# Sliding-window attention and a two-layer network on one core: the first tiles of a half, steps 5 to 11, a mask and four loads are placed anew

## The chip, the cores and the metric

The kernel runs on one core of a Trainium2 chip. A core has five engines, each with its own queue of instructions in program order: TensorE (PE in the profile; its weight loads are shown apart as PEld), VectorE (DVE), ScalarE (ACT), GpSimd (POOL) and SyncE (SP). SP computes nothing here and only starts transfers; POOL starts some too. An engine does its instructions in order, and one that waits holds up all behind it. The metric is the device time of the kernel in microseconds (us), as a median of several runs.

## The reference

```python
def _attn_ref(q, k, v):                     # 8 batches, 8 heads, 576 tokens, 64 wide
    scores = scale * np.matmul(q, k.transpose(0, 1, 3, 2))
    mask = np.abs(pos[:, None] - pos[None, :]) <= 32
    scores = np.where(mask, scores, -1000000000.0)
    scores = scores - np.max(scores, axis=-1, keepdims=True)
    attn = np.exp(scores)
    attn = attn / (np.sum(attn, axis=-1, keepdims=True) + 1e-09)
    return np.matmul(attn, v)
...
def _moe_ref(x, w_in, w_out):               # x: 4608 x 512, d_ff 2048
    h = x @ w_in
    g = np.maximum(0.01 * h, h)
    return g @ w_out
```

Each token sees 65 neighbours at most. The heads of a token, side by side, are a row of x.

## The kernel before

Two heads make a pair: 4 pairs a batch, 8 batches, and each batch's 576 tokens are cut into two halves of 288. So there are 64 *steps*, numbered i; `where(i)` gives batch i // 8, half (i // 4) % 2 and pair i % 4. `g`, from 0 to 15, numbers the halves in the network.

**One step.** `score(i)` makes 5 matmuls (L276) into the one PSUM tile `ps`, ACT takes the exponent `e` out of it (L281), and POOL multiplies `e` with the mask of the half, `mask[0]` or `mask[1]`, into `prob` (L283). `sums(i)` adds up the keys by a matmul with ones (L302 where DVE has first joined two parts into `both`, L293, from step 12 on; L305, two matmuls, before), and DVE takes the reciprocal `r` (L310). `product(i)` makes 5 matmuls with the values (L321) into the one PSUM tile `x`, and DVE writes `xT`, x times r (L335). `step()` issues for step i, in this order: the join of i+1, the scores of i+2, sums, product and xT of i, and then what falls due: keys put in place (`place_keys`, DVE, L259 or L261), casts of q and k of a later batch (`cast_qk`, L198), their transposes by DMA (L213) and loads.

**Operands.** q, k and v come in fp32 as `qf`, `kf`, `vf`, one buffer for each pair, so a load waits for the cast of the batch before. Batches 0 and 1 are transposed by PE (`transposes`, L226) and taken out by ACT (L234, L240); later ones by DMA on SP's queue. The values of a pair are cast into `vbd`, of batch 1 by ACT (`cast_v` with `on_act`, L204, two instructions a pair), of later ones by POOL (L206). Keys go into `kbd`; both are double buffers by batch.

**Network.** `h_tile(g, f)` makes 4 matmuls (L349), one for each pair of heads c, into a PSUM tile of the pool `mm` (4 buffers), and ACT writes gT (L356). 16 tiles f make a half. `h_first` does the first four f at once, c by c, for g = 0 and 1. `o_tile(j)` makes 16 matmuls (L388) for 128 tokens, ACT copies them to `o_sb` (L393), SP stores them (L394).

**Order.** The order is written out by hand: up to step 7 and half g = 1 line by line, with `second_half()` for steps 4 to 7 between the tiles of g = 0, and `second_pair(p)`, which transposes pair p of batch 1 (on PE), between tiles of g = 1. From there a plan of quarter o tiles (4 matmuls, counted O_US = 0.864) and h tiles (H_US = 0.49) is walked through; `spend` is called before each piece and issues the next step when the planned clock has come to its `due` time. The plan opens with four o tiles (16 quarters, n = 0 to 15), then the 16 h tiles of g = 2. Before quarters 0 and 3 `spend` also calls `second_pair(2)` and `second_pair(3)`, and after the latter ACT casts the values of pair 0 of batch 1; the cast of pair i-7 goes out with step i for i = 8, 9, 10.

**Loads of a later batch.** In `step()` `qk_due` casts and transposes pair p of batch 2 in step 9 + p, of batch b > 2 in step 8 (b-1) + p + 2, and loads pair p of the batch after at once; `v_due` does the same for values.

```python
    LEAD = 4.0                                             # L566, with H_US and O_US
    due = []
    for i in range(8, NC):
        prev = 0.75 * O_US * 4 if i < 12 else at[i // 4 - 1] - LEAD + (1.8 if i < 16 else 0)
        due.append(prev + (at[i // 4] - LEAD + (1.8 if i < 12 else 0) - prev) * (i % 4 + 1) / 4)
```

`at[g]` is the planned time of the first h tile of half g. With these dues steps 8, 9, 10, 11 go out before the quarters n = 6, 9, 11 and 14.

Of the kernel before, what the change touches and what calls it, by code (L numbers as in the profile page):

```python
# [9 lines left out]
FP32 = mybir.dt.float32  # L10
# [6 lines left out]
def kernel(  # L17
# [14 lines left out]
    nc = tc.nc  # L32

    B, H, S, D = q.shape
# [5 lines left out]
    NPAIR = H // 2  # L40
    NB = S // 64
    HALF = S // 2
    DMC = DMODEL // 128
    FFC = DFF // 128
    EVEN = HALF // 2
# [12 lines left out]
    mmps = ctx.enter_context(tc.tile_pool(name="mmps", bufs=4, space=PS))  # L58
# [9 lines left out]
    def load_qk(b, p, behind=None):  # L68

        for into, src, name in ((qf, q, "qf"), (kf, k, "kf")):
            t = fload.tile([96, 2, RUN * D], FP32, name=f"{name}{p}")
            if behind is not None:
                behind.memset(t[0:1, 0, 0:1], 0.0)
                behind = None
            heads = src[b, 2 * p:2 * p + 2]
            if b < BY_DMA:
                nc.sync.dma_start(out=t, in_=heads.rearrange("a (p c) d -> p a (c d)", c=RUN))
            else:  # L80
                nc.sync.dma_start(
                    out=t.rearrange("p a (g e) -> p a g e", g=3),
                    in_=heads.rearrange("a (g p c) d -> p a g (c d)", g=3, c=2),
                )
            into[b, p] = t
# [45 lines left out]
    mask = [const.tile([128, 2, 2, EVEN], BF16, name=f"mask{i}") for i in range(2)]  # L131
# [16 lines left out]
    for lo in (0, 64):  # L148
        w = win[lo:lo + 64]
        nc.gpsimd.affine_select(  # L150
            out=w, in_=w, compare_op=ALU.is_ge, fill=0.0,
# [3 lines left out]
            out=w, in_=w, compare_op=ALU.is_ge, fill=0.0,  # L155
# [2 lines left out]
    nc.gpsimd.memset(vbd[0][:, 3], 0.0)  # L158
    win_f = win.rearrange("p c m i -> p c (m i)")

    def make_masks():
        for hf in range(2):
            lo = (16, 32)[hf]
            nc.gpsimd.tensor_copy(out=mask[hf][:, 0], in_=win_f[:, :, lo:lo + EVEN])
            lo = (16, 0)[hf]
            nc.gpsimd.tensor_copy(out=mask[hf][:, 1, :, lo:lo + 128], in_=win_f[:, :, 0:128])

    NPROB = 6
    prob = const.tile([128, NPROB, 2, 2, EVEN], BF16)
# [5 lines left out]
        out=ps[:, 512:512 + HALF], in_=zero.to_broadcast([128, HALF]), func=AF.Copy,  # L175
# [11 lines left out]
    def cast_qk(b, p, q_eng=None):  # L187
        for eng, src, dst in ((q_eng or nc.gpsimd, qf, qb), (nc.gpsimd, kf, kb)):
            if b < BY_DMA:
                parts = [(dst[:, p], src[b, p].rearrange("p a (c d) -> p c a d", d=D))]  # L190
            else:
                by_c = src[b, p].rearrange("p a (g c d) -> c p g a d", g=3, c=2)
                parts = [(dst[:, p, 3 * c:3 * c + 3], by_c[c]) for c in range(2)]
            for to, tok in parts:
                if eng is nc.scalar:
                    eng.activation(out=to, in_=tok, func=AF.Copy)
                else:
                    eng.tensor_copy(out=to, in_=tok)  # L198

    def cast_v(b, p, on_act=False):  # L200
        for a in range(2):
            r = slice(64 * a, 64 * a + 64)
            if on_act:
                nc.scalar.activation(out=vbd[b % 2][r, p, :, r], in_=vf[b, p][r], func=AF.Copy)  # L204
            else:
                nc.gpsimd.tensor_copy(out=vbd[b % 2][r, p, :, r], in_=vf[b, p][r])  # L206
# [42 lines left out]
    def place_keys():  # L249

        while landing and landing[0][0] <= state["done"]:
            unplaced.append(landing.pop(0)[1:])
        while unplaced:
            b, p, kT = unplaced.pop(0)
            for a in range(2):
                r = slice(64 * a, 64 * a + 64)
                to = kbd[b % 2][r, p, :, r]
                if b < BY_DMA:
                    nc.vector.tensor_copy(out=to, in_=kT[r].rearrange("p (n j) -> p n j", j=64))  # L259
                else:  # L260
                    nc.vector.tensor_copy(  # L261
                        out=to.rearrange("p n (m c) -> p n c m", c=2),
                        in_=kT[r].rearrange("p (c n m) -> p n c m", c=2, n=NB),
                    )
# [6 lines left out]
    def score(i):  # L271
        b, hf, p = where(i)
        by_c = qT[b][:, p].rearrange("p (c i) -> p c i", c=2)
        for n_, blocks in enumerate(WIN[hf]):
            for blk, i0, n in blocks:
                nc.tensor.matmul(  # L276
                    ps_v[:, n_, :, i0:i0 + n], kbd[b % 2][:, p, blk],
                    by_c[:, :, hf * EVEN + i0:hf * EVEN + i0 + n], start=True, stop=True,
                )
        e = attn.tile([128, 2 * HALF], BF16, name="e")  # L280
        nc.scalar.activation(out=e, in_=ps[:, P0:P0 + 2 * HALF], func=AF.Exp, scale=scale)  # L281
        pr = prob[:, i % NPROB]
        nc.gpsimd.tensor_mul(  # L283
            pr.rearrange("p n c i -> p (n c i)"), e, mask[hf].rearrange("p n c i -> p (n c i)"),
        )
        probs[i] = [pr, None, None]

    def join(i):


        pr = probs[i][0].rearrange("p n c i -> p n (c i)")
        both = joined.tile([128, HALF], BF16, name="both")
        nc.vector.tensor_add(both, pr[:, 0], pr[:, 1])  # L293
        probs[i][1] = both
# [42 lines left out]
    def weighted(i):  # L337
        if probs[i][2] is None:
            sums(i)
        product(i)  # L340
        scaled(i)
# [5 lines left out]
    def h_mms(g, f, h, cs):  # L347
        for c in cs:
            nc.tensor.matmul(  # L349
                h[:, 0:HALF], w_in_bf[:, c, ts(f, 128)], xT[:, c, ds(g * HALF % RING, HALF)],  # L350
                start=(c == 0), stop=(c == DMC - 1),
            )

    def h_out(g, f, h):

        nc.scalar.activation(  # L356
            out=gT[:, f, ds(g * HALF % RING, HALF)].rearrange("p (i c) -> p i c", c=2),
            in_=h[:, 0:HALF].rearrange("p (c i) -> p i c", c=2), func=AF.Prelu, alpha=0.01,
        )

    def h_tile(g, f):

        h = mmps.tile([128, 512], FP32, name="mm", tag="mm")
        h_mms(g, f, h, range(DMC))
        h_out(g, f, h)

    def h_first(g):

# [37 lines left out]
    NC = 2 * NPAIR * B  # L406
# [11 lines left out]
    def step():  # L418


        i = state["done"]
        if JOINED - 1 <= i < NC - 1:
            join(i + 1)
        if i < NC - 2:
            score(i + 2)
        weighted(i)
        place_keys()
        for b, p in qk_due.get(i, ()):
            cast_qk(b, p)
            transpose_dma(b, p)  # L430
            if b + 1 < B:
                load_qk(b + 1, p)
        for b, p in v_due.get(i, ()):
            cast_v(b, p)
            if b + 1 < B:
                load_v(b + 1, p)
        state["done"] += 1
# [5 lines left out]
    def load_w_in(f0, f1):  # L443
        nc.gpsimd.dma_start(out=w_in_bf[:, :, f0:f1], in_=w_in_r[:, :, f0:f1])
# [10 lines left out]
        place_keys()  # L455

    cast_qk(0, 0, nc.vector)
    make_masks()
    cast_qk(0, 1, nc.vector)
    first_pair()  # L460
    first_pair()
# [19 lines left out]
    next(first)  # L481
    cast_v(0, 1, on_act=True)
    load_w_in(1536, 2048)
    place_keys()
    keep_busy(ps, 0, 8)
    sums(2)
# [7 lines left out]
    h = next(h0)  # L494
# [34 lines left out]

    for f in range(4, FFC):  # L530
        h_tile(0, f)
        if f in (6, 10, 13):
            second_half()
        if f % 2 == 1:
            nc.gpsimd.memset((kbd if f < 12 else vbd)[1][:, (f - 4) // 2 % 4], 0.0)
# [30 lines left out]
    H_US, O_US, LEAD = 4 * (HALF / 2400 + 2.5e-3), 4 * 0.216, 4.0  # L566
# [8 lines left out]
    at, t = {}, 0.0  # L575
    for us, kind, g, f in plan:
        if kind == "h" and f == 0:
            at[g] = t
        t += us
    due = []  # L580
    for i in range(8, NC):
        prev = 0.75 * O_US * 4 if i < 12 else at[i // 4 - 1] - LEAD + (1.8 if i < 16 else 0)
        due.append(prev + (at[i // 4] - LEAD + (1.8 if i < 12 else 0) - prev) * (i % 4 + 1) / 4)
    clock = 0.0
    turn = 0

    def spend(us):
        nonlocal clock, turn
        while due and due[0] <= clock:
            due.pop(0)  # L590
            i = state["done"]
            if i < 11:
                cast_v(1, i - 7, on_act=True)
            step()
            if 10 <= i < 14:
                load_v(2, i - 10)
        turn += 1
        if turn == 1:
            second_pair(2)
        if turn == 2:  # L600
            score(9)
        if turn == 4:
            second_pair(3)
            cast_v(1, 0, on_act=True)
        clock += us

    for us, kind, g, f in plan:
        if kind == "h":
            spend(us)
            h_tile(g, f)  # L610
        elif f == 0:
            o_tile(g, lambda: spend(O_US))
# [28 lines left out]
```

## Time and profile before

| | |
|---|---|
| median of 9 runs | 321.02 us (320.43 to 321.72) |
| profiled execution | 321.11 us |
| its span, first to last instruction | 319.4 us |
| granted TensorE clock | 1.00 |
| DVE, share of the span | 69% |
| POOL, ACT, share of the span | 60%, 58% |
| HBM read, written | 36.70 MB, 9.44 MB |

The profiled execution's own time is 1.7 us above its span, which is what lies before the first and after the last instruction. Times within the profile are counted from the start of the span. Matmuls are pipelined: the profile shows one 128x288 matmul at 0.286 us, but 16 of them issued back to back take 1.96 us in the chain of waits, 0.1225 us each; four 128x512 ones take 0.863 us (0.2158 each), the five of a score or product 0.24 us. These issue times are used below.

### The profile page before, as it was taken

How to read it: one execution, taken by the hardware profiler on the slowest of the kernel's cores; microseconds unless marked ns; L12 is line 12 of the kernel's file. 1: busy time of each engine (PE TensorE's matmuls, PEld its weight loads, DVE VectorE, ACT ScalarE, POOL GpSimd, SP SyncE). 2: the span in 40 equal slices, each digit the busy share in tenths (PEclk: the TensorE clock that was granted, in tenths of full speed). 3: DMA queues.
4: the chain of work that ended last, by engine and by line, in shares of the span. 5: the costliest groups of instructions: out<-in, count | busy, mean ns of one | idle time of the engine just before them, and what ended most of it. 6: DMA issues, size and time to landing. Idle time of an engine off the chain costs nothing.

```text
span 319.4 us, 6459 instructions
## 1 busy us (share of the span) xinstructions
PE 301.5 (94%) x2429; PEld 203.6 (64%) x2449; DVE 220.6 (69%) x259; ACT 184.5 (58%) x393; POOL 191.7 (60%) x251
## 2 busy tenths in 40 slices
PE   1679999999999999999999999999999999999996
PEld 1467765575755858576665858576665857576653
DVE  5788885889555987688745987688745988565100
ACT  7587688584642828475552838465552837464531
POOL 8888963894356866586637866586637866330000
PEclk9999999999999999999999999999999999999999
DMA  8999999999996998399934996399733440000102
GB/s 194 221 180 223 268 242 209 261 198 224 202 222 137 237 188 176 76 236 178 201 76 113 229 227 157 74 217 243 156 76 104 107 72 33 33 37 2 66 29 72
DMA packets 108400, 49.46 MB, mean 155 GB/s; under 512 B 68816, under 2 KB 103888, under 8 KB 108368
## 3 DMA queue, kind: packets, MB, share of 16 engines
q1 hardware_dynamic: 104144, 44.84, 67.5%
q0 software_dynamic: 4224, 4.19, 8.0%
q8 instruction: 19, 0.31, 0.4%
q14 instruction: 13, 0.11, 0.1%
HBM read 36.70 MB, written 9.44 MB: 144 GB/s over the span
## 4 chain that ended last, share of the span: by engine, by line
PE 81%; DVE 6%; DMA 3%; ACT 3%; POOL 3%; issue 2%; SPq 0%; POOLq 0%; DVEq 0%; ACTq 0%
PE mm L349 35%; PE mm L388 34%; PE x L321 4%; PE ps L276 4%; DVE r L310 4%; DMA kf<-in_k_dram 2%; PE s L302 2%; POOL prob L283 2%; DMA kT<-kb 2%; DVE qb L198 1%; DVE xT L335 1%; ACT vbd L204 1%; ACT e L281 1%; PE s L305 1%; PE tp L226 1%
## 5 line engine op out<-in xcount | busy, mean ns | idle before, releaser
L310 DVE RECIPROCAL r<-s 128x288 f32<-128x288 f32 x64 | 125.2, 1956 | 52.5 <-PE s L302 49.9
L349 PE MATMUL mm<-xT,w_in_bf 128*128 128x288 bf16 x1024 | 134.2, 286 | 0.7 <-DVE xT L335 0.4
L283 POOL TENSOR_TENSOR prob<-e,mask 128x576 bf16<-128x576 bf16 x64 | 81.7, 1276 | 86.2 <-ACT e L281 43.7
L388 PE MATMUL mm<-w_out_bf,gT 128*128 128x512 bf16 (+2 forms) x572 | 128.7, 373 | 1.1
L356 ACT ACTIVATE gT<-mm 128x288 bf16<-128x288 f32 x256 | 103.7, 412 | 25.0 <-PE mm L349 6.3
L349 PEld LDWEIGHTS <-w_in_bf 128*128 128x128 bf16 x1024 | 98.4, 98 | 25.4 <-issue 1.3
L388 PEld LDWEIGHTS <-gT 128*128 128x128 bf16 x592 | 56.3, 98 | 59.3
L393 ACT ACTIVATE o_sb<-mm 128x512 f32<-128x512 f32 (+2 forms) x37 | 21.7, 585 | 89.1 <-PE mm L388 89.1
L281 ACT ACTIVATE e<-ps 128x576 bf16<-128x576 f32 x64 | 41.4, 648 | 10.8 <-PE ps L276 10.6
L206 POOL CAST vbd<-vf 64x576 bf16<-64x576 f32 x50 | 34.3, 686 | 5.1 <-DMA vf<-in_v_dram 3.5
L198 POOL CAST kb<-kf 96x384 bf16<-96x384 f32 (+1 forms) x56 | 35.1, 650 | 3.7 <-DMA kf<-in_k_dram 3.6
L335 DVE TENSOR_TENSOR xT<-x,r 128x288 bf16<-128x288 f32 x64 | 29.3, 458 | 8.7 <-PE x L321 1.7
L261 DVE COPY kbd<-kT 64x576 bf16<-64x576 bf16 x48 | 32.2, 670 | 4.0 <-DMA kT<-kb 3.7
L276 PE MATMUL ps<-qT,kbd 128*128 128x128 bf16 (+2 forms) x320 | 26.2, 214 | 1.8 <-DVE kbd L259 1.2
L276 PEld LDWEIGHTS <-kbd 128*128 128x128 bf16 x320 | 20.8, 99 | 10.6 <-DVE kbd L259 1.5
L321 PE MATMUL x<-prob,vbd 128*128 128x128 bf16 (+2 forms) x320 | 26.0, 213 | 0.9 <-DVE xT L335 0.6
L198 POOL CAST qb<-qf 96x384 bf16<-96x384 f32 x48 | 24.4, 536 | 0.0
L321 PEld LDWEIGHTS <-vbd 128*128 128x128 bf16 x320 | 20.6, 99 | 3.8 <-issue 1.2
L293 DVE TENSOR_TENSOR both<-prob 128x288 bf16<-128x288 bf16 x52 | 19.2, 370 | 1.6 <-POOL prob L283 0.8
L302 PE MATMUL s<-both,ones_bd 128*128 128x288 bf16 x52 | 14.9, 286 | 0.3 <-DVE r L310 0.3
L198 DVE CAST qb<-qf 96x768 bf16<-96x768 f32 x7 | 10.8, 1556 | 1.6 <-DMA qf<-in_q_dram 1.5
L259 DVE COPY kbd<-kT 64x576 bf16<-64x576 bf16 x16 | 7.1, 442 | 5.9 <-ACT kT L240 5.8
(43 smaller groups left out, 82.1 us busy)
## 6 DMA issues: line engine op xcount, KB each, us to landing
qf<-in_q_dram SPq DMA_DIRECT2D x32, 288.0 KB, 4.6
kf<-in_k_dram SPq DMA_DIRECT2D x32, 288.0 KB, 5.3
vf<-in_v_dram SPq DMA_DIRECT2D x64, 144.0 KB, 5.0
out_dram<-o_sb SPq DMA_DIRECT2D x35, 256.0 KB, 4.0
w_in_bf<-in_moe_w_in_dram POOLq DMA_DIRECT2D x4, 512.0 KB, 8.4
w_out_bf<-in_moe_w_out_dram POOLq DMA_DIRECT2D x4, 512.0 KB, 16.3
qT<-qb SPq DMA_TRANSPOSE x24, 4.0
kT<-kb SPq DMA_TRANSPOSE x24, 3.2
```

Source lines behind the costliest of these rows:

```text
L198: eng.tensor_copy(out=to, in_=tok)
L206: nc.gpsimd.tensor_copy(out=vbd[b % 2][r, p, :, r], in_=vf[b, p][r])
L261: nc.vector.tensor_copy(out=to.rearrange("p n (m c) -> p n c m", c=2), in_=kT[r].rearrange("p (c n m) -> p n c m", c=2, n=NB),)
L276: nc.tensor.matmul(ps_v[:, n_, :, i0:i0 + n], kbd[b % 2][:, p, blk], by_c[:, :, hf * EVEN + i0:hf * EVEN + i0 + n], start=True, stop=True,)
L281: nc.scalar.activation(out=e, in_=ps[:, P0:P0 + 2 * HALF], func=AF.Exp, scale=scale)
L283: nc.gpsimd.tensor_mul(pr.rearrange("p n c i -> p (n c i)"), e, mask[hf].rearrange("p n c i -> p (n c i)"),)
L310: nc.vector.reciprocal(r, s)
L321: nc.tensor.matmul(x_v[:, :, i0:i0 + n], vbd[b % 2][:, p, blk, :], pr[:, n_, :, i0:i0 + n], start=(blk == parts[0][1]), stop=(blk == parts ...
L335: nc.vector.tensor_mul(place(i), x, r)
L349: nc.tensor.matmul(h[:, 0:HALF], w_in_bf[:, c, ts(f, 128)], xT[:, c, ds(g * HALF % RING, HALF)], start=(c == 0), stop=(c == DMC - 1),)
L356: nc.scalar.activation(out=gT[:, f, ds(g * HALF % RING, HALF)].rearrange("p (i c) -> p i c", c=2), in_=h[:, 0:HALF].rearrange("p (c i) -> ...
L388: nc.tensor.matmul(o[:, lo:hi], gT[:, f, ds(128 * j % RING, 128)], w_out_bf[:, f, lo:hi], start=(f == 0), stop=(f == FFC - 1),)
```

## The change

1. `make_masks()` becomes `make_mask(hf)`: the mask of the first half is still built on POOL after the first cast of k; that of the second half follows the issue of the last w_in load.
2. In half g = 0 `second_half()` (steps 4 to 7) is called after tiles f = 5, 9, 13 instead of 6, 10, 13. The last call of it is where it was.
3. `h_tile` can do two tiles at once: three matmuls of the one, three of the other, then the last pair's matmul of each, then both to ACT. It does so for f = 0 and 1 of every half from g = 2 on.
4. The dues of steps 8 to 11 are given in quarters: n = 4, 7, 10, 12 in place of 6, 9, 11, 14. Those of later steps stay.
5. Loads of q and k of batch 3 leave steps 9 to 12 (where batch 2 is cast) and go out in steps 13 to 16, behind that step's key placement. Nothing else is loaded elsewhere.

Everything that is computed stays. On DVE the order of instructions is the same; on PE the steps stand elsewhere among the tiles, on ACT one `e` goes ahead of one gT and a cast of values ahead of one `o_sb`, on POOL the two mask copies move and one memset goes behind `prob` of step 7.

```diff
-    def make_masks():
-        for hf in range(2):
-            lo = (16, 32)[hf]
-            nc.gpsimd.tensor_copy(out=mask[hf][:, 0], in_=win_f[:, :, lo:lo + EVEN])
-            lo = (16, 0)[hf]
-            nc.gpsimd.tensor_copy(out=mask[hf][:, 1, :, lo:lo + 128], in_=win_f[:, :, 0:128])
+    def make_mask(hf):
+        lo = (16, 32)[hf]
+        nc.gpsimd.tensor_copy(out=mask[hf][:, 0], in_=win_f[:, :, lo:lo + EVEN])
+        lo = (16, 0)[hf]
+        nc.gpsimd.tensor_copy(out=mask[hf][:, 1, :, lo:lo + 128], in_=win_f[:, :, 0:128])
...
-    def h_tile(g, f):
-        h = mmps.tile([128, 512], FP32, name="mm", tag="mm")
-        h_mms(g, f, h, range(DMC))
-        h_out(g, f, h)
+    def h_tile(g, f, n=1):
+        hs = [mmps.tile([128, 512], FP32, name="mm", tag="mm") for _ in range(n)]
+        for cs in (range(DMC - 1), (DMC - 1,)) if n > 1 else (range(DMC),):
+            for i, h in enumerate(hs):
+                h_mms(g, f + i, h, cs)
+        for i, h in enumerate(hs):
+            h_out(g, f + i, h)
...
         for b, p in qk_due.get(i, ()):
             cast_qk(b, p)
             transpose_dma(b, p)
-            if b + 1 < B:
+            if 2 < b < B - 1:
                 load_qk(b + 1, p)
+        if 12 < i <= 12 + NPAIR:
+            load_qk(3, i - 13)
...
     cast_qk(0, 0, nc.vector)
-    make_masks()
+    make_mask(0)
...
     load_w_in(1536, 2048)
+    make_mask(1)
     place_keys()
...
-        if f in (6, 10, 13):
+        if f in (5, 9, 13):
             second_half()
...
-    due = []
-    for i in range(8, NC):
-        prev = 0.75 * O_US * 4 if i < 12 else at[i // 4 - 1] - LEAD + (1.8 if i < 16 else 0)
-        due.append(prev + (at[i // 4] - LEAD + (1.8 if i < 12 else 0) - prev) * (i % 4 + 1) / 4)
+    due = [O_US * n for n in (4, 7, 10, 12)]
+    for i in range(12, NC):
+        prev = at[i // 4 - 1] - LEAD + (1.8 if i < 16 else 0)
+        due.append(prev + (at[i // 4] - LEAD - prev) * (i % 4 + 1) / 4)
...
-        while due and due[0] <= clock:
+        while due and due[0] <= clock + 1e-6:
...
         if kind == "h":
             spend(us)
-            h_tile(g, f)
+            if f != 0:
+                h_tile(g, f - 1, 2) if f == 1 else h_tile(g, f)
```

## The prediction

> **What bounds the kernel now.** I read the page first, then a table of busy time by windows, then the waits of PE, and last the timeline around each of them.
>
> ```profile
> PE 301.5 (94%) x2429; PEld 203.6 (64%) x2449; DVE 220.6 (69%) x259; ACT 184.5 (58%) x393; POOL 191.7 (60%) x251
> ```
> ```profile
> 92.00:316.00 224.00, 223.21 (x1742) 148.52 (x1755) 150.23 (x176) 119.96 (x266) 124.00 (x164) 1.00 0.60 129
> ```
>
> The first number after the window is its length, the second PE's busy time. PE is the bound, and from 92 us on it is busy 223.21 of 224 us at a clock of 1.00. Nothing in the last 228 us can get shorter while the same matmuls are issued. What can be won lies before 92, where PE waits. The change touches little before 25 us (below), so I look at 25 to 92:
>
> ```profile
> PE tp L226 <- DVE qb L198: 0.5, 1, 0.5
> PE s L305 <- DVE r L310: 0.5, 1, 0.5
> PE mm L349 <- DVE xT L335: 0.4, 1, 0.4
> PE s L302 <- DVE r L310: 0.3, 1, 0.3
> PE x L321 <- DVE xT L335: 0.3, 1, 0.3
> ```
>
> Five single waits. Modelled ends of matmuls hide part of each, so I price a wait as the distance of two starts less the issue time of what lies between (0.1225 us for a 288-column matmul, 0.24 for five of a step).
>
> ```profile
> 32.72 0.40 PE L321 MATMUL x<-prob,vbd 128*128 128x64 bf16 x5
> 33.59 0.42 PE L305 MATMUL s<-prob,ones_bd 128*128 128x288 bf16 x2 [0.46 <-DVE r L310]
> ...
> 43.56 1.14 PE L349 MATMUL mm<-xT,w_in_bf 128*128 128x288 bf16 x8
> 45.22 0.43 PE L226 MATMUL tp<-ident,qb 96*128 96x96 bf16 x6 [0.52 <-DVE qb L198]
> ...
> 63.53 0.53 PE L349 MATMUL mm<-xT,w_in_bf 128*128 128x288 bf16 x3
> 64.49 1.26 PE L349 MATMUL mm<-xT,w_in_bf 128*128 128x288 bf16 x9 [0.43 <-DVE xT L335]
> ...
> 87.26 0.40 PE L276 MATMUL ps<-qT,kbd 128*128 128x96 bf16 x5
> 87.97 0.28 PE L302 MATMUL s<-both,ones_bd 128*128 128x288 bf16 x1 [0.31 <-DVE r L310]
> 88.54 0.40 PE L321 MATMUL x<-prob,vbd 128*128 128x96 bf16 x5 [0.28 <-DVE xT L335]
> ```
>
> So: W1, step 7's sums, 33.59 - 32.72 - 0.24 = 0.63. W2, transposes of pair 2, 45.22 - 43.56 - 0.98 = 0.68. W3, last pair of g = 2, 64.49 - 63.53 - 0.37 = 0.59. W4, 87.97 - 87.26 - 0.24 = 0.47 and 88.54 - 87.97 - 0.12 = 0.45. One of 0.30 at 57.9 (product of step 10 behind xT) is W5.
>
> **The masks: 0.** At the old place POOL's next work was held by a transfer anyway (the cast of k at 8.41 waited 0.32 for kf). At the new place POOL stands idle 0.77 us for `e` (20.22 to 21.00). The two copies cost 0.42 + 0.39; the worst row of the second is 0.72. So `prob` of step 3 slips 0.04 to 0.4. It ended at 22.26, and its sums run at 22.70. Behind it in POOL's queue are a w_out load, `prob` of step 4 (needed at 25.28, done at 24.35) and the loads of q and k from 25.2; they slip as much, within cover. Without that cover it would be the 0.4.
>
> **Second halves: W1 shrinks by 0.50.** Steps 4 and 5 go one tile (0.49) earlier. Product 4 moves 28.08 to 27.60, xT 4 to 28.03 (r 4 ends at 27.69); sums 5 are done at 28.25, so r 5 runs 28.4 to 30.36 (1.95 each). Product 5 moves to 30.28, is done 0.40 later, xT 5 runs to 31.17, r 6 ends at 33.03 in place of 33.53. Step 6's product stays at 32.72, so sums 7 start at 33.09: 0.13 is left of 0.63. r 7 and xT 7 follow 0.5 sooner, and so does g = 1. Score 7, also 0.49 sooner, finds `ps` just free (`e` 6 ends at 28.02). Bounds 0.3 (if it doesn't) to 0.63.
>
> **W2 goes: 0.68.** The cast for which PE waited:
>
> ```profile
> 42.09 3.07 DVE L198 CAST qb<-qf 96x768 bf16<-96x768 f32 x1
> 41.94 0.82 POOL L198 CAST kb<-kf 96x768 bf16<-96x768 f32 x1 [2.31 <-DMA kf<-in_k_dram]
> 42.70 2.05 POOL L559 MEMSET vbd<- 128x1152 bf16 x2
> ```
>
> The same DVE cast took 0.68 at 7.16, and here 3.07, as long as POOL works beside it. POOL's start is set by a transfer, so it stays near 41.94. DVE's start is set by PE and ACT (keys of pair 0), which come 0.5 sooner: 41.60, now ahead of POOL. Priced at 0.68, DVE ends at 42.3 and POOL's cast by about 43.1, both before PE arrives (44.54 - 0.50 = 44.04). Priced at 3.07 it ends at 44.7, leaving 0.5 of gain at that point; if it still ends when POOL is done, at 45.16, W1's gain is lost too. I take 0.68, since DVE starts first by 0.34. PE then transposes pair 3 at T = 48.57 - 1.18 = 47.39. k of pair 3 lands at 45.7, its cast ends at 46.56, in time; the last part of w_out (issued 29.3, 18.7 to landing: 48.0) holds the next matmuls by 0.1, inside the next wait.
>
> The Trainium skill, "SBUF — State Buffer", section "Who interferes with whom", says that a DVE cast in a two-port mode and a POOL instruction exclude each other, and that the one issued first has the ports for its whole length. The 3.07 above fits it only if POOL's three instructions all went ahead. By that rule alone the start order would settle the 0.68; the trace has no case of a DVE start 0.3 ahead of a POOL chain.
>
> **Steps 8 to 11: a new wait, net +0.66.** ACT casts the values of pair 0 after taking out pair 3:
>
> ```profile
> 50.25 1.39 ACT L204 ACTIVATE vbd<-vf 64x576 bf16<-64x576 f32 x2
> 51.66 0.60 ACT L393 ACTIVATE o_sb<-mm 128x512 f32<-128x512 f32 x1
> 52.28 1.39 ACT L204 ACTIVATE vbd<-vf 64x576 bf16<-64x576 f32 x2
> ```
>
> The cast ends 51.64 - 48.57 = 3.07 after T. Before, step 8's product came 52.16 - 48.57 = 3.59 after T, with three quarters between. Now only one quarter lies there: transposes 0.51, quarter 0.86, scores 0.24, sums 0.25, that is T + 1.86. PE waits until T + 3.11: 1.25 lost, with all PE work queued behind. From there, on ACT: o_sb, values of pair 1 by T + 5.10, `e` 10 by T + 5.77, values of pair 2 by T + 7.18, `e` 11 by 7.85, values of pair 3 by 9.88, `e` 12 by 10.55. PE: step 9 at T + 5.94, step 10 at T + 9.26, step 11 at T + 11.71, each after what it needs. r 10 runs T + 9.95 to 11.9, xT 10 to 12.46, so product 11 waits 0.32. Then four quarters (3.45): g = 2 starts at T + 16.21. POOL's casts of batch 2 hold `prob` of step 12, and so the join ahead of r 11, until T + 12.5; xT 11 is done by T + 15.6, so W3 and W5 are gone. Before, g = 2 effectively started at 63.53 + 0.59 = 64.12 = T + 15.55. Sum: + 1.25 + 0.32 - 0.59 - 0.30 = +0.68, by the starts +0.66. Bounds: +0.3 (the casts of pair 0 found sooner) to +1.3 (another such wait).
>
> **Pairs of tiles: 0.** They let xT of a last pair come 0.37 later. g = 2 no longer waits by the sum above (if xT 11 is late by up to that, it is covered), and from 92 on no half waits. Their cost: ACT gets the first tile 0.37 later; its buffer is drained about 1.6 after the start and wanted at 1.96.
>
> **Loads of batch 3: W4 goes, 0.91.**
>
> ```profile
> 84.16 1.56 DVE L261 COPY kbd<-kT 64x576 bf16<-64x576 bf16 x2 [3.46 <-DMA kT<-kb]
> 85.97 1.95 DVE L310 RECIPROCAL r<-s 128x288 f32<-128x288 f32 x1
> ```
>
> Keys of batch 2's last pair came late: SP issued the transpose at 79.13, and behind it DVE's reciprocals ran late into W4. SP had been held by eight loads of 288 KB between the transposes. Without them the cast that feeds the last transpose ends at about T + 22.4 = 69.8, the transpose goes out by 72.4 and lands, with 5.0 as now, by 77.4; DVE wants it at 80.7. The loads now follow, on a queue behind them only stores and values; they land some 5 to 10 us after steps 13 to 16 (69 to 82) and are cast in steps 18 to 21 (from 93 on). Bounds 0.4 to 0.91.
>
> **Sum:** -0.50 - 0.68 + 0.66 - 0.91 = -1.43 us. The span goes 319.4 to 318.0, the profiled execution 321.11 to 319.7; the median is 0.09 below that execution, so 319.6.
>
> **Rivals.**
> A. *The cast is still held by POOL.* k lands a third of a us earlier, or DVE starts no sooner; for it, the trace's one long cast. PE is then at T = 48.2 to 48.57: -0.37 to 0 in place of -1.18, sum -0.62 to -0.25: 320.4 to 320.8. Chance 0.2.
> B. *Slower: step 8 is pinned to the landing of v.* The second half of v for pair 0 was issued at 33.69 and landed 15.1 us later, at 48.8; ACT would now like to begin its cast at T + 1.68 = 49.07. A landing later by s moves product 8 and all behind it by s - 0.27; with -0.52 at the start of g = 2 (63.60 against 64.12) and W4's 0.91 the kernel gets slower from s = 1.7 on, measurably from 2.35. Pair 2 of v lands 3.8 us after pair 0 now; if pair 0 came as late, the sum is +2.1. So 321.7 to 323.1. Against it: the queue carries the same bytes until then. Chance 0.1.
> C. *The keys are late still*, as the transposes are held by something other than those loads (stores, values): W4 stays, -0.5: 320.5. Against it, 3.3 us of slack. Chance 0.13.
>
> **How the numbers follow.** Forecast 0.57; A 0.2, B 0.1, C 0.13. The forecast's own spread: best W1 0.63, step 8 at +0.3: -1.9; worst W1 0.3, W2 0.5, wait +1.0, W4 0.7: -0.5. So 319.0 to 320.9 holds it with A and C. A measurement can tell 0.2% (0.64 us) from no change: faster (below 320.4) the forecast and a third of A and C, 0.67; same 0.23; slower, B, 0.1.
>
> **What would show it.** Right: sums 7 wait 0.1; the DVE cast takes under 1.5 us and PE transposes pair 2 without a wait; a new wait of PE (L321) on ACT's vbd (L204) of 1.2 before 51; g = 2 without a wait; no wait of DVE L261 on kT near 84. Wrong: the cast again near 3 us, or a wait that isn't listed, above all PE on DVE in g = 2.

## The result, and the profile after

| | before | changed |
|---|---|---|
| median, both on the same chip | 321.25 us (63 runs) | 319.88 us (21 runs) |
| ratio, 95% interval | | 0.9955 (0.9946 to 0.9964) |
| profiled execution | 321.11 us | 319.79 us |
| its span | 319.4 us | 318.1 us |

The changed kernel is 0.45% faster: 1.45 us by the ratio, 1.37 between the medians, 1.32 between the profiled executions. The forecast was 1.43 us less, 319.6. The page's busy line and the table by windows of the changed kernel come first (in the table: window, its length, busy time and count of PE, PEld, DVE, ACT and POOL, then granted clock, DMA share and GB/s).

```profile
PE 303.1 (95%) x2429; PEld 205.1 (64%) x2449; DVE 218.3 (69%) x259; ACT 182.4 (57%) x393; POOL 191.2 (60%) x251
```
```profile
25.00:64.00 39.00, 37.55 (x328) 25.42 (x329) 28.98 (x32) 27.97 (x61) 29.35 (x36) 1.00 1.12 232
64.00:92.00 28.00, 27.90 (x234) 19.90 (x234) 21.01 (x26) 17.77 (x41) 16.09 (x21) 1.00 1.04 208
92.00:314.00 222.00, 221.21 (x1723) 147.24 (x1736) 150.60 (x176) 117.84 (x265) 124.00 (x164) 1.00 0.60 132
```

PE still has 0.8 us without work in the last window, as before (there over 224 us): nothing was won after 92, and the clock is 1.00 in all three. Between 64 and 92 it is now busy 27.90 of 28 us. Next come the waits of PE from 25 to 95 us, the whole answer of that view, and PE's timeline (start, duration, engine, line, operation, tiles, shape, count, idle time before it and what ended it).

```profile
PE mm L390 <- DMA w_out_bf<-in_moe_w_out_dram: 0.8, 1, 0.8
```
```profile
32.81 0.40 PE L320 MATMUL x<-prob,vbd 128*128 128x64 bf16 x5
33.18 0.42 PE L304 MATMUL s<-prob,ones_bd 128*128 128x288 bf16 x2
...
43.16 1.14 PE L348 MATMUL mm<-xT,w_in_bf 128*128 128x288 bf16 x8
44.14 0.42 PE L225 MATMUL tp<-ident,qb 96*128 96x96 bf16 x6
...
47.48 0.42 PE L225 MATMUL tp<-ident,qb 96*128 96x96 bf16 x6
47.97 0.43 PE L225 MATMUL tp<-ident,kb 96*128 96x96 bf16 x6
49.21 1.02 PE L390 MATMUL mm<-w_out_bf,gT 128*128 128x512 bf16 x4 [0.81 <-DMA w_out_bf<-in_moe_w_out_dram]
...
50.31 0.41 PE L304 MATMUL s<-prob,ones_bd 128*128 128x288 bf16 x2
50.60 0.41 PE L320 MATMUL x<-prob,vbd 128*128 128x96 bf16 x5
...
63.76 1.63 PE L348 MATMUL mm<-xT,w_in_bf 128*128 128x288 bf16 x12
...
86.90 0.40 PE L275 MATMUL ps<-qT,kbd 128*128 128x96 bf16 x5
87.14 0.29 PE L301 MATMUL s<-both,ones_bd 128*128 128x288 bf16 x1
87.26 0.40 PE L320 MATMUL x<-prob,vbd 128*128 128x96 bf16 x5
```

By the same reading as before (distance of two starts less issue time): W1 is 33.18 - 32.81 - 0.24 = 0.13. W2 is gone: eight matmuls of 0.1225 fill 43.16 to 44.14. Twelve fill 63.76 to 65.23 in the same way, so g = 2 doesn't wait, and at 87 nothing is left between scores, sums and product. The only wait the view lists wasn't priced as one: the last part of w_out landed near 49.2. Transposes and casts of the same execution follow.

```profile
41.69 0.56 DVE L197 CAST qb<-qf 96x768 bf16<-96x768 f32 x1
```
```profile
43.00 0.82 POOL L197 CAST kb<-kf 96x768 bf16<-96x768 f32 x1 [2.58 <-DMA kf<-in_k_dram]
```
```profile
49.15 1.39 ACT L203 ACTIVATE vbd<-vf 64x576 bf16<-64x576 f32 x2
```

The cast that took 3.07 takes 0.56. And the transfer of w_out hides the forecast's new wait: ACT has the values at 50.54, step 8's product starts at 50.60, just after its sums. Without the transfer it would have waited from T + 1.86 = 49.34, so the two together cost 1.26, what the one was priced at (1.25). Here k of pair 3 came late too (its transposes 0.23 later than the 0.26 issue time asks); that was inside the same cover, and no other profile has it.

**One table for all kernels.** Three marks cut each profiled execution: S, the first matmul of g = 0 (L348 or L349); T, the transposes of pair 3, as in the prediction; H, the start of g = 2's matmuls plus the wait ahead of their last pair, if there is one. "To the end" is the span less H.

| kernel | S | S to T | T to H | H to the end |
|---|---|---|---|---|
| before | 22.94 | 25.63 | 15.55 | 255.28 |
| changed | 23.02 | 24.46 | 16.28 | 254.34 |
| changed, second profile (after_again) | 22.94 | 24.44 | 16.22 | 254.30 |
| u_loads | 22.62 | 24.45 | 16.21 | 255.42 |
| u_second | 22.64 | 25.70 | 16.21 | 254.35 |
| u_dues | 22.09 | 24.45 | 15.46 | 254.40 |
| u_dues, second profile (dues_again) | 22.46 | 24.45 | 15.48 | 254.31 |
| u_mask | 22.73 | 24.45 | 16.21 | 254.31 |
| u_pair | 22.62 | 24.45 | 16.22 | 254.31 |
| a_second | 23.07 | 24.46 | 15.57 | 256.30 |
| a_dues | 22.89 | 25.48 | 16.22 | 254.71 |
| a_loads | 22.97 | 25.74 | 15.54 | 254.35 |
| dues_single | 23.02 | 24.46 | 15.54 | 254.38 |
| best3 | 22.41 | 25.26 | 14.95 | 254.38 |

The first stretch of the change holds W1 and W2, the second steps 8 to 11, the third W4. S wanders by up to 0.98 us between profiles. It follows POOL's second cast of k, which starts once its k has landed and POOL's mask copies are done: S comes 14.40 to 14.69 after that start in thirteen of the fourteen profiles, 14.68 or 14.69 in eight of them (15.19 in the changed kernel's first, where PE also waited for values). Of the five parts only the masks lie ahead of S (see u_mask).

### The profile page after: what moved, and what is told of

It reads as the page before. It is cut to its first block, busy times and chain, and to the rows that moved or that the text cites. A ratio compares the mean times of both kernels' runs of the same rounds, so it can differ in the third digit from the quotient of the medians.

```text
span 318.1 us, 6454 instructions
## 1 busy us (share of the span) xinstructions
PE 303.1 (95%) x2429; PEld 205.1 (64%) x2449; DVE 218.3 (69%) x259; ACT 182.4 (57%) x393; POOL 191.2 (60%) x251
## 4 chain that ended last, share of the span: by engine, by line
PE 84%; DMA 8%; DVE 2%; ACT 2%; POOL 1%; issue 1%; SPq 0%; ACTq 0%; DVEq 0%; POOLq 0%
PE mm L390 37%; PE mm L348 35%; DMA w_out_bf<-in_moe_w_out_dram 6%; PE x L320 4%; PE ps L275 4%; PE s L301 2%; DVE r L309 2%; DMA kf<-in_k_dram 2%; PE s L304 1%; ACT e L280 1%; POOL prob L282 1%; PE ps L402 1%; DVE xT L334 0%; SPq L79 0%; ACT vbd L203 0%
## 5 line engine op out<-in xcount | busy, mean ns | idle before, releaser
L348 PE MATMUL mm<-xT,w_in_bf 128*128 128x288 bf16 x1024 | 134.0, 286 | 0.3
L355 ACT ACTIVATE gT<-mm 128x288 bf16<-128x288 f32 x256 | 101.2, 412 | 24.9 <-PE mm L348 8.4
L348 PEld LDWEIGHTS <-w_in_bf 128*128 128x128 bf16 x1024 | 98.4, 98 | 24.8 <-issue 0.6
L225 PE MATMUL tp<-ident,qb 96*128 96x96 bf16 x48 | 4.4, 243 | 5.9 <-DVE qb L197 5.7
```

What stands on the lines that cost most here:

```text
L348: nc.tensor.matmul(h[:, 0:HALF], w_in_bf[:, c, ts(f, 128)], xT[:, c, ds(g * HALF % RING, HALF)], start=(c == 0), stop=(c == DMC - 1),)
L355: nc.scalar.activation(out=gT[:, f, ds(g * HALF % RING, HALF)].rearrange("p (i c) -> p i c", c=2), in_=h[:, 0:HALF].rearrange("p (c i) -> ...
```

## The experiments

Names that begin with u_ undo one part of the changed kernel, names that begin with a_ put one part alone into the kernel before; after_again and dues_again are repeats, dues_single and best3 change two things at once. Each ratio is to the kernel before on the same chip, whose medians lay between 321.02 and 321.12 us in these runs.

**The loads back in steps 9 to 12 (u_loads).**

```diff
-            if 2 < b < B - 1:
+            if b + 1 < B:
                 load_qk(b + 1, p)
-        if 12 < i <= 12 + NPAIR:
-            load_qk(3, i - 13)
```

> The changed kernel with the loads of q and k of batch 3 back in steps 9 to 12. My theory (these loads, between the transposes of batch 2 on SP's queue, make the last pair's keys late): the changed kernel plus 0.9 us, 320.8, and in the profile a wait of DVE's key copy (L260) on kT near 84 us, with waits of PE on DVE of together 0.9 us near 88. Rival (with steps 8 to 11 earlier the transposes go out earlier anyway): 319.9 to 320.2 and no such wait.

320.59 us, ratio 0.9985 (0.9972 to 0.9997): 0.0030 more than the changed kernel's, about 0.96 us. Its DVE and PE timelines:

```profile
83.36 1.69 DVE L260 COPY kbd<-kT 64x576 bf16<-64x576 bf16 x2 [3.54 <-DMA kT<-kb]
```
```profile
86.42 0.40 PE L275 MATMUL ps<-qT,kbd 128*128 128x96 bf16 x5
87.31 0.28 PE L301 MATMUL s<-both,ones_bd 128*128 128x288 bf16 x1 [0.48 <-DVE r L309]
87.87 0.40 PE L320 MATMUL x<-prob,vbd 128*128 128x96 bf16 x5 [0.28 <-DVE xT L334]
```

The keys are late again, and W4 is back with 0.65 + 0.44 = 1.09; the third stretch says 1.12 (255.42 against 254.30). SP issues the last transpose of keys at 78.14 here and at 74.51 in the changed kernel; this is the row of each, u_loads first:

```profile
78.14 1.21 SPq L212 DMA_TRANSPOSE kT<-kb  x1
```
```profile
74.51 1.21 SPq L212 DMA_TRANSPOSE kT<-kb  x1
```

It lands 5.2 us after its issue here (83.3) and 2.5 us after it in the changed kernel (77.0). C has fallen: those loads are the cause.

**The loads alone (a_loads).** The same edit the other way round, in the kernel before.

> The kernel before with the loads of q and k of batch 3 in steps 13 to 16, and nothing else changed. My theory: minus 0.9 us, ratio 0.997 (0.9965 to 0.9978), no wait of DVE's key copy on kT near 84 us. Rival (the transposes stay late behind stores and values): minus 0.3 us at most.

319.84 us, ratio 0.9968 (0.9954 to 0.9982), 1.03 us less. W1 to W3 stand (0.63, 0.79, 0.59) and W4 is gone, 0.93 of the third stretch.

**The second halves back after tiles 6, 10, 13 (u_second).**

```diff
-        if f in (5, 9, 13):
+        if f in (6, 10, 13):
```

> The changed kernel with the second halves back after tiles 6, 10 and 13. My theory (the earlier steps let DVE's cast of q of pair 2 start ahead of POOL): step 7's sums wait 0.6 us again, and where k of pair 2 lands ahead of DVE's start the cast takes 3 us: plus 0.5 to 1.2 us, 320.4 to 321.1. Rival (the last part of w_out, landing at 48.0 to 49.2, holds PE at the fourth quarter of the first o tile in any case): the loss upstream is taken out of that wait, plus 0 to 0.2 us, 319.9 to 320.1, with the wait on w_out shorter than its 0.97 us in the changed kernel.

320.40 us, ratio 0.9983 (0.9971 to 0.9995), 0.0028 more: about 0.90 us. Its DVE and POOL timelines:

```profile
41.79 3.14 DVE L197 CAST qb<-qf 96x768 bf16<-96x768 f32 x1
```
```profile
41.70 0.82 POOL L197 CAST kb<-kf 96x768 bf16<-96x768 f32 x1 [2.38 <-DMA kf<-in_k_dram]
```

DVE starts 0.09 after POOL and takes 3.14; W1 (0.63) and W2 (0.75) are back, and the first stretch is longer by 1.25. S lay 0.3 to 0.4 earlier than in the changed kernel's profiles, which can be why the time shows only 0.90.

**The second halves alone (a_second).** The same edit the other way round.

> The kernel before with the second halves after tiles 5, 9 and 13, and nothing else changed. My theory (0.5 us from step 7's sums, and 0.6 to 0.7 more where DVE's cast of q of pair 2 then starts ahead of POOL's cast of k): minus 1.1 us, ratio 0.9965 (0.9955 to 0.9975), the cast at 0.56 us instead of 3.1. Rival (the first gain is swallowed by the wait for w_out or by the wait for xT at half 2): minus 0 to 0.4 us.

320.92 us, ratio 0.9989 (0.9976 to 1.0001): no change that can be told, where the theory had 1.1 us less. This expectation failed, and the table says where: the first stretch did shorten, by 1.17, and the third is 1.02 longer. Its PE, DVE and POOL timelines at that place:

```profile
80.25 0.53 PE L349 MATMUL mm<-xT,w_in_bf 128*128 128x288 bf16 x3
81.61 0.77 PE L349 MATMUL mm<-xT,w_in_bf 128*128 128x288 bf16 x5 [0.82 <-DVE xT L335]
```
```profile
76.63 1.05 DVE L261 COPY kbd<-kT 64x576 bf16<-64x576 bf16 x2 [1.01 <-DMA kT<-kb]
77.72 1.41 DVE L293 TENSOR_TENSOR both<-prob 128x288 bf16<-128x288 bf16 x1
```
```profile
77.68 1.28 POOL L283 TENSOR_TENSOR prob<-e,mask 128x576 bf16<-128x576 bf16 x1 [1.71 <-ACT e L281]
```

In the kernel before, DVE's rows at this place were:

```profile
76.87 1.05 DVE L261 COPY kbd<-kT 64x576 bf16<-64x576 bf16 x2 [0.23 <-DMA kT<-kb]
77.95 0.31 DVE L293 TENSOR_TENSOR both<-prob 128x288 bf16<-128x288 bf16 x1
```

PE comes to this half a us earlier, but the transposed keys don't (SP issues their transpose at 72.74, before at 72.99): DVE waits 1.01 for them instead of 0.23. The join behind them then starts 0.04 after POOL's `prob` and takes 1.41 instead of 0.31. PE waits 81.61 - 80.25 - 0.37 = 0.99 for xT, and W4 (0.47 + 0.44) follows as ever. So the gain of this edit is only kept where the keys' transposes aren't held up. The parts don't add: alone, this one is worth 0.13 by the three stretches, which the time can't tell from nothing; on top of the moved loads it is worth 0.9.

**The quarters back at 6, 9, 11, 14 (u_dues, and again as dues_again).**

```diff
-    due = [O_US * n for n in (4, 7, 10, 12)]
+    due = [O_US * n for n in (6, 9, 11, 14)]
```

> The changed kernel with steps 8 to 11 back before the quarters 6, 9, 11 and 14. My theory as in the forecast's sum (the early step 8 costs a wait of 1.25 us on ACT's cast of the values and saves 0.9): minus 0.3 to 0.7 us, 319.2 to 319.6. Rival (PE waits for the last part of w_out just ahead of step 8, so that the wait on the cast is hidden in it, and the earlier steps only save the waits ahead of half 2): plus 0.2 to 0.6 us, 320.1 to 320.5, with a wait of PE on xT (L334) at the start of half 2.

318.23 us, ratio 0.9922 (0.9908 to 0.9936): 1.06 us below the changed kernel, by ratios, where the theory gave 0.3 to 0.7 and the rival a loss. The sign was right, the size was missed. Both were run once more on one chip, with a second profile of each.

> The changed kernel once more, as the measure for the other runs beside it: ratio 0.9955 to the kernel before, and in the profile the wait of about 1.25 us on ACT's cast of values at step 8 where the last part of w_out lands near 48 us, less where it lands later. Against it stands that the wait seen in its first profile, on w_out, is the rule.

> The changed kernel with the old quarters 6, 9, 11, 14, once more. My theory (the new quarters cost 1.25 + 0.32 and save 0.30 + 0.23 us): 1.0 us under the changed kernel on the same chip, ratio 0.9923. Rival (0.5 us of its first result came from an early start of that run, its second k landing 1.1 us sooner): 0.4 to 0.7 us under it, ratio 0.9935 to 0.994.

The changed kernel took 319.21 us (ratio 0.9945, 0.9925 to 0.9964) and the one with the old quarters 318.44 (0.9917, 0.99 to 0.9934): 0.77 us apart by the medians, 0.90 by the ratios, between the theory's 1.0 and the rival's 0.4 to 0.7. The stretches decide: S differs by 0.48, the second stretch by 0.74, the others by 0.01. So the rival was right that a part is an early start; 0.74 belongs to the quarters. Of the changed kernel's second profile these are PE and ACT:

```profile
47.64 0.42 PE L225 MATMUL tp<-ident,kb 96*128 96x96 bf16 x6
48.38 1.02 PE L390 MATMUL mm<-w_out_bf,gT 128*128 128x512 bf16 x4 [0.32 <-DMA w_out_bf<-in_moe_w_out_dram]
...
49.48 0.41 PE L304 MATMUL s<-prob,ones_bd 128*128 128x288 bf16 x2
50.50 0.41 PE L320 MATMUL x<-prob,vbd 128*128 128x96 bf16 x5 [0.62 <-ACT vbd L203]
```
```profile
49.06 1.39 ACT L203 ACTIVATE vbd<-vf 64x576 bf16<-64x576 f32 x2
```

Here w_out came earlier, and the wait named in the prediction shows: 50.50 - 49.48 - 0.24 = 0.78, and 48.38 - 47.64 - 0.26 = 0.48 for w_out, 1.26 together (1.25 forecast). In u_loads, u_second and a_dues, where w_out was in time, the product alone waits 1.25. And PE of dues_again:

```profile
47.17 0.42 PE L225 MATMUL tp<-ident,kb 96*128 96x96 bf16 x6
47.72 2.75 PE L390 MATMUL mm<-w_out_bf,gT 128*128 128x512 bf16 x12
50.31 0.40 PE L275 MATMUL ps<-qT,kbd 128*128 128x96 bf16 x5
50.55 0.41 PE L304 MATMUL s<-prob,ones_bd 128*128 128x288 bf16 x2
50.79 0.40 PE L320 MATMUL x<-prob,vbd 128*128 128x96 bf16 x5
...
62.16 1.86 PE L348 MATMUL mm<-xT,w_in_bf 128*128 128x288 bf16 x12
63.86 0.40 PE L275 MATMUL ps<-qT,kbd 128*128 128x64 bf16 x5
```

Twelve matmuls lie ahead of step 8, its product waits for nothing, and g = 2 waits 63.86 - 62.16 - 1.47 = 0.23. The second stretch is 15.48 against 16.22: the new quarters cost 0.74 us. This is the best of the kernels run, in both of its runs.

**The new quarters alone (a_dues).** The quarters 4, 7, 10, 12 in the kernel before.

> The kernel before with steps 8 to 11 ahead of the quarters 4, 7, 10 and 12, and nothing else changed. My theory (a wait of 1.25 us on ACT's cast of the values of pair 0 of batch 1, and 0.3 in step 11, against 0.9 of waits saved): plus 0.6 us, ratio 1.002 (1.001 to 1.003). Rival (earlier steps bring the casts and transposes of batch 2 forward, so the keys of its last pair come in time near 84 us): minus 0.2 to 0.4 us.

321.38 us, ratio 1.0013 (1.0000 to 1.0026), where the theory had 1.002. The second stretch is 0.67 longer, as the theory has it, and 0.57 comes back in the third, which it had left out: PE reaches W4 later, and 0.38 is left of it. The first stretch is 0.15 shorter, so the three together are 0.05 shorter than before; whether the part is a loss on its own isn't shown.

**The old quarters with single tiles (dues_single), the changed kernel with single tiles (u_pair).** Both have this edit, dues_single beside that of u_dues:

```diff
-            if f != 0:
-                h_tile(g, f - 1, 2) if f == 1 else h_tile(g, f)
+            h_tile(g, f)
```

> The changed kernel with steps 8 to 11 at the old quarters and the first two tiles of a half one after the other: the kernel before with the second halves, the loads of batch 3 and the mask moved. My theory (putting the last pair's matmuls behind two tiles covers 0.36 of the 0.59 us that half 2 waits for xT with the old quarters; with 6, 9, 11, 14 and pairs 0.23 was left): 0.36 us above the version with pairs, ratio 0.9933 against 0.9922, and a wait of 0.59 us (rather than 0.23) on xT at the start of half 2. Rival (the pairs do nothing): equal to the version with pairs, ratio 0.992.

319.42 us, ratio 0.9949 (0.9933 to 0.9964). Its PE timeline at g = 2:

```profile
62.43 0.53 PE L348 MATMUL mm<-xT,w_in_bf 128*128 128x288 bf16 x3
63.39 1.26 PE L348 MATMUL mm<-xT,w_in_bf 128*128 128x288 bf16 x9 [0.43 <-DVE xT L334]
```

The wait is 63.39 - 62.43 - 0.37 = 0.59, with pairs of tiles it was 0.23: they take 0.36, three matmuls, when the old quarters leave a wait there. The median is above u_dues' by more than that, 0.87 us by the ratios; S was 0.93 and 0.56 later than in the two profiles of u_dues, which can be the rest.

> The changed kernel with the first two tiles of a half one after the other. My theory: within 0.15 us of the changed kernel, since with the new quarters xT of step 11 is ready before half 2 and no later half waits. Rival (the pairs cover something at half 2 with the new quarters too): plus 0.3 us, with a wait on xT near 63.

319.74 us, ratio 0.9962 (0.9946 to 0.9978), where the changed kernel beside it had 0.9945 (0.9925 to 0.9964). The intervals overlap, so the time alone leaves it open. In the profile g = 2 starts without a wait at T + 16.22, as with the pairs: the two parts of the change cover the same wait.

**Both masks at the old place (u_mask).**

```diff
     make_mask(0)
+    make_mask(1)
...
     load_w_in(1536, 2048)
-    make_mask(1)
     place_keys()
```

> The changed kernel with both masks built at the old place. My theory (both places lie in idle time of POOL): within 0.15 us of the changed kernel, 319.7 to 320.0. Rival (the two copies at the new place, or their absence at the old one, shift the transfers of w_in and w_out, whose last part landed 1.2 us later in the changed kernel's profile): the last part of w_out lands near 48.0 us again and the time falls by 0.3 to 0.8 us; or, if the old place holds up the second cast of k, it rises by as much.

319.58 us, ratio 0.9963 (0.9951 to 0.9976): the changed kernel's within the intervals. All three stretches are those of its second profile within 0.01, but the masks lie ahead of S, where these can't show them. POOL's rows can, of u_mask and then of u_dues, which has one mask there:

```profile
7.70 0.39 POOL L165 COPY mask<-win 128x256 bf16<-128x256 bf16 x1
8.04 0.82 POOL L197 CAST kb<-kf 96x768 bf16<-96x768 f32 x1
```
```profile
7.06 0.39 POOL L165 COPY mask<-win 128x256 bf16<-128x256 bf16 x1
7.41 0.82 POOL L197 CAST kb<-kf 96x768 bf16<-96x768 f32 x1
```

In both the second cast of k starts right behind the copies, with no wait for the transfer. With both masks ahead of it, it started at 8.04 to 8.50 (five profiles), with one at 7.41 to 8.34 (nine, six of them before 8.04), and S is 14.69 and 14.68 behind it in the two shown. So the moved mask costs nothing at its new place and can gain up to 0.6 us where k lands early; where k lands after 8.04 it gains nothing. What that is worth on the median these runs don't settle.

**Old quarters, and three tiles at once at g = 2 (best3).** On top of u_dues, to take away the last 0.23:

```diff
-            if f != 0:
-                h_tile(g, f - 1, 2) if f == 1 else h_tile(g, f)
+            n = 3 if g == 2 else 2
+            if f >= n - 1:
+                h_tile(g, 0, n) if f == n - 1 else h_tile(g, f)
```

> The changed kernel with the old quarters and, in half 2, the first three tiles at once. My theory: the 0.23 us that are left of the wait for xT at half 2 go, since a third tile adds 0.37 of cover: 0.2 us under the version with two, no wait of PE on xT near 62. Rival (ACT gets its first tile 0.37 later still and the tiles behind wait for a buffer): equal or slower by up to 0.2.

A median of 318.47 us, but from 317.71 to 322.02 over 12 runs, four of them above 321; ratio 0.9945 (0.9914 to 0.9976). Inconclusive, and why four runs lie 3 us higher stays open. Its profile, on DVE, POOL and PE:

```profile
41.08 3.19 DVE L197 CAST qb<-qf 96x768 bf16<-96x768 f32 x1
```
```profile
41.04 0.82 POOL L197 CAST kb<-kf 96x768 bf16<-96x768 f32 x1 [1.96 <-DMA kf<-in_k_dram]
```
```profile
42.55 1.14 PE L348 MATMUL mm<-xT,w_in_bf 128*128 128x288 bf16 x8
44.32 0.43 PE L225 MATMUL tp<-ident,qb 96*128 96x96 bf16 x6 [0.63 <-DVE qb L197]
...
62.62 1.63 PE L348 MATMUL mm<-xT,w_in_bf 128*128 128x288 bf16 x12
```

The wait at g = 2 is gone, as meant. But k of pair 2 landed early for DVE (POOL's cast starts 18.63 after S here, 19.28 in dues_again), POOL was 0.04 ahead of DVE, the cast took 3.19, and PE waited 44.32 - 42.55 - 0.98 = 0.79 for it. This is the prediction's rival A, in a kernel that has the second halves at their new place.

## Why the prediction was right

**By stretches.** The prediction had S to T 1.18 shorter, T to H at 16.21 in place of 15.55, and 0.91 less after that. The two profiles of the changed kernel have 1.17 and 1.19; 16.28 and 16.22; 0.94 and 0.98. That its medians came within 0.1 us of the forecast is in part luck, since S alone can move a profile by more.

- *Masks, 0:* not settled. At the new place `prob` of step 3 still waited 0.58 for `e` in the changed kernel, so nothing was lost there. At the old place the forecast saw the transfer hold POOL anyway, which is so in the profile before, but not where k lands earlier (u_mask).
- *W1, 0.50:* 0.50. The forecast left 0.13 of it; so does the trace.
- *W2, 0.68:* gone in every profile in which DVE started its cast first, and there in every one in which POOL did. T came at 47.48 and 47.38 (47.39 forecast). Only the price of a free cast was a little high: 0.56 measured, 0.68 taken from another row, at 7.16, beside POOL's mask copies; it lies under cover.
- *Steps 8 to 11, +0.66:* right in size and place (1.25 for product 8, 0.30 for product 11 where 0.32 was summed, no W3, no W5). That w_out "holds the next matmuls by 0.1, inside the next wait" was right in kind: it held them by 0.98 and 0.48, without cost, since the values were later still.
- *Pairs of tiles, 0:* right in this kernel. What the sum, taken part by part, couldn't show is that this zero depends on the part before it: with the old quarters they are worth 0.36, and so the new quarters cost 0.74 in the kernel that is left, not 0.66. (With pairs the old quarters' second stretch would be 15.55 - 0.36 = 15.19; w_out, no longer covered there, takes 0.29 back: 15.48, and 15.46 and 15.48 are measured.)
- *Loads of batch 3, 0.91:* 0.94 and 0.98; a_loads alone 0.93 (the two waits in the forecast add up to 0.92). Two misses cancel: the last transpose of keys left SP at 74.51, not by 72.4, behind two loads of values and a store, but landed 2.5 us later, not 5.0, so at 77.0 where 77.4 was forecast; DVE's copy at 80.22 waits for nothing. And of the eight loads named, six lay between the transposes before: the last pair's own two went out behind its transpose (at 80.39 and 81.02).

**The rivals.** A didn't come in the changed kernel (DVE was ahead by 1.31 and 0.35 us), but hangs on a start order that best3 lost by 0.04 us and u_dues won by 0.07; 0.2 was not too much for it. B didn't come: ACT's cast at 49.15 and 49.06 follows its own `kT` copy, which starts at 48.48 and 48.39 and takes 0.65, not the landing of v. In the first profile the second half of v landed at 49.4, later than the cast began; only the second of the cast's two instructions, from about 49.8, reads it, so B's slack was larger than the 0.27 it was given. C was excluded by u_loads and a_loads.

**The rule of the Trainium skill.** "SBUF — State Buffer", section "Who interferes with whom", gives the port pair to whichever of the two instructions is issued first. The runs agree as far as the order decides: POOL first by 0.04, 0.09 and 0.15 us gave 3.19, 3.14 and 3.07 for the cast, DVE first by 1.31 gave 0.56. The closest case is u_dues: DVE first by 0.07 gave 0.56 too, and there POOL's cast took 1.17 instead of 0.82. They differ in the length: DVE was held through three POOL instructions (0.82 + 2.05), not through one.

## What to carry to other kernels

Cut a trace at a few marks on the bounding engine and compare the stretches: here they repeated to some 0.1 us wherever PE met the same waits, while medians also carried a wandering start of up to 1 us. But a part that lies ahead of the first mark, as the mask did, needs a mark of its own. Ask of every part of a change what it is worth after the others are in: the moved second halves paid only with the moved loads, and the new quarters bought nothing that the pairs of tiles hadn't already, so undoing them gave a kernel 0.74 us faster than the changed one. A gain that depends on which of two engines starts first needs its margin looked up, since 0.04 us on the wrong side cost 0.79.

## What the runs showed that had not been expected

- A bf16 join of DVE (128x288, usually 0.31 us) took 1.41 when it started 0.04 after POOL's 1.28 us `prob` of bf16 (a_second): DVE's casts from fp32 aren't the only ones that are held.
- The start of the network's first matmul (S) lay anywhere from 22.09 to 23.07 us in kernels whose work up to there is all but the same. It followed the start of POOL's second cast of k (7.41 to 8.50); why that k lands when it does wasn't tried.
- The last part of w_out landed between 47.3 and 49.2 us in kernels that differ little ahead of it. It cost nothing in the changed kernel, 0.29 in both profiles of u_dues, and nothing in dues_single and best3, where it had landed before PE came.
